# Expert rows written in 512-byte pieces and read in 2 KB pieces, late weight splits in an expert's first unit, and another order of splits and routing in the first unit

## The chip, the cores and the metric

The kernel runs on one core of a Trainium2 chip. The engines that matter here are PE (matmuls), ACT and DVE (elementwise work), POOL (gathers and scatters by index) and SP (which here issues the ordinary DMAs). Each of them takes its instructions in the order in which they stand in its own program. The metric is the device time of one execution in microseconds (us): the median of three runs before was 791.21 us (790.51 to 791.55).

## The reference

Linear attention over 8 batches x 8 heads x 576 positions x 64, then a mixture of experts over the 4608 rows of 512 that the attention gives. Each row goes to the one expert with the highest cosine similarity:

```python
expert_idx = np.argmax(logits, axis=1)
gate_w = probs[np.arange(N), expert_idx]
for e in range(E):
    mask = expert_idx == e
    if not mask.any():
        continue
    h = np.maximum(x[mask] @ w1[e], 0.0)          # 512 -> 1024
    out[mask] = gate_w[mask, None] * (h @ w2[e])  # 1024 -> 512
```

With the given inputs the reference sends 540, 5, 574, 0, 1152, 1759, 0 and 578 rows to the experts 0 to 7.

## The kernel before, in words

**Attention** fills the first 300 us or so. It is followed by the **experts**, in units of at most 384 rows, all of one expert. The order of the experts is worked out on the chip: the largest expert goes first, then the others in cyclic order. Here that gives unit 0 (384 rows of expert 5), units 1 to 5 (the rest of expert 5), 6 and 7 (expert 7), 8 and 9 (expert 0), 10 (the 5 rows of expert 1), 11 and 12 (expert 2) and 13 to 16 (expert 4). Unit 0 is written out (`first_unit`, `first_layers`) and is interleaved with the last routing steps. Every other unit is one of 14 **arms** of a switch (`ARMS`, L33): a size, whether the unit is the first of its expert, whether it is the last. Engines jump into an arm at the unit's start and out of it near its end; the rest of the unit (`unit_end`) is common to all arms. So unit 10 is the only one here whose arm is both first and last. Its 5 rows are computed 256 wide in the first layer (L760) and as two slots in the second.

**Precision.** Weights and rows are held as a high and a low part. `wsplit(0, c)` splits chunk c of 8 of w1, `wsplit(1, c)` chunk c of w2: ACT copies the raw weights `w1r` or `w2r` into the high part, DVE subtracts (L586 to L591). Layer 1 of a chunk is 12 matmuls (L696), followed by a relu on ACT (`high`, L698) and a subtraction on DVE (`low`, L701) that free its PSUM bank; five banks take turns. Layer 2 is three matmuls a slot and chunk (L718).

**Weights.** A first unit (t > 1) asks at chunk 1 for the second half of w1 and the first half of w2 of the next expert, and at chunk 5 for the second half of w2 (L765 to L771). A last unit asks for the first half of w1 of the expert after that (`next_w1`, L721). A last unit splits the next expert's w1 chunk by chunk as its own layer 1 leaves them free (L776, c from 2 to 9) and w2's chunks 0 to 3 (L796, c from 5 to 8); w2's chunks 4 to 7 are split in the expert's first unit (L763). Arms that are not last carry tiny instructions in the same places instead (`idle`, L808), on DVE and ACT.

**Rows.** The rows of unit t+2 are gathered by POOL into `raw` (`collect`, three gathers at chunks 0 to 2), written by SP to the DRAM tensor `xr` (`put`, chunk 4) and read back in another order into `xg` (`fetch`, chunk 7), which needs `put` to have landed. In the next unit, at chunks 5 and 6, DVE transposes `xg` in 32 x 32 blocks into `xt` (`turned`, L626), and `xsplit` makes the high and low parts of the rows for the unit after. `put` is one DMA with runs of 2 KB; `fetch` is four DMAs, one for each group of 32 partitions, with runs of 512 bytes.

**Unit 0.** Three of w1's chunks (5 to 7) are split in `first_layers` at c = 0, 1, 2 (`w1_chunk`, L733). The last routing steps stand at numbered places of the same loop (`extras`, L1052): `norms` at 0, `logits` at 2, `choice` at 4, and at 9 `rest`: `count` (four small matmuls on PE, L434 and L435), `ranks`, `tables` (which unit is which arm), then w2's chunks 4 to 7, the table scatters, and the gathers for unit 1. In this part the order on ACT, DVE, POOL and SP is chosen when the program is built, by the order in which the work is written and by planned costs; only PE's order is written by hand. Within the arms all orders are written by hand.

Of the kernel before, what the change touches and what calls it, by code (L numbers as in the profile page):

```python
# [20 lines left out]
P = 128  # L21
B, H, S, HD = 8, 8, 576, 64
K = 3
# [8 lines left out]
LAG, CUT = 5, 5  # L32
# [80 lines left out]
class Kernel:  # L113
# [382 lines left out]
    def tables(self):  # L496
# [4 lines left out]
        v, cst, tab = self.v, self.cst, self.tab  # L501
        pool = self.pb
        it, ie = cst[:, C_IT:C_IT + 1], cst[:, C_IE:C_IE + E]
        es = self.es

        def t_(name, shape, dt_=F32):
            return pool.tile([P] + shape, dt_, name="t_" + name)

        ci, hi = t_("ci", [E], I32), t_("hi", [E], I32)
        s, c, half, odd, one, nu, few = (t_(n, [E]) for n in ("s", "c", "half", "odd", "one", "nu", "few"))  # L510
# [29 lines left out]
        def one_hot(name, t):  # L540
            a, b = t_(name + "a", [E]), t_(name, [E])
            v.tensor_scalar(out=a, in0=cum, scalar1=t, scalar2=None, op0=ALU.is_gt)
            v.scalar_tensor_tensor(out=b, in0=st, scalar=t, in1=a, op0=ALU.is_le, op1=ALU.mult)
            return b

        def pick(name, m, vals):
            a, r = t_(name + "a", [E]), t_(name, [1])
            v.tensor_tensor(out=a, in0=m, in1=vals, op=ALU.mult)
            v.tensor_reduce(out=r, in_=a, axis=AX.X, op=ALU.add)
            return r  # L550
# [22 lines left out]
        mn = one_hot("mn", ce)  # L573
        v.tensor_copy(out=tab[:, 2:3], in_=pick("nx", mn, ie))
        mn = one_hot("mo", pick("cf", mn, cum))
        v.tensor_copy(out=tab[:, 0:1], in_=pick("ny", mn, ie))

# [27 lines left out]
            self.after(ins, first, mybir.DependencyClass.Sync, "spread over the unit")  # L607

    def put(self, t):
        self.nc.sync.dma_start(out=self.rowsd(t).rearrange("(s p) d -> p s d", p=P), in_=self.raws)  # L610

    def fetch(self, t):

        rows = self.rowsd(t).rearrange("(s i) (g d) -> g i s d", i=32, g=4)
        for g in range(4):
            self.nc.sync.dma_start(out=self.xgs[32 * g:32 * g + 32].rearrange("i s (q d) -> i (s q) d", q=4), in_=rows[g])

    def ordered(self, slots, engines):

# [107 lines left out]
    def first_layers(self, n, extra):  # L727

        self.late_tiles()
        for c in range(8 + LAG):  # L730
            late = c - LAG + 1
            if c < 8:
                self.w1_chunk()  # L733
                if c < 4:
                    self.wsplit(1, c, self.nc.gpsimd)
                hidden = self.layer1(0, c, n, c % 2 if c > 1 else 2 + c)
                if c == 4:
                    self.after(hidden[1], self.counts, mybir.DependencyClass.NoSync, "the count is waited for")
            extra(2 * c)
            if late == 6:  # L740
                self.arms = {1: self.arm(1)}
                self.ordered(3, [self.act_copy, self.dve_copy, self.act_copy])
                self.tc.switch_hint(self.arms[1], len(ARMS), label="unit1")
            if late >= 7:
                self.xtr(1, 3, range(3 * late - 21, min(3 * late - 18, 4)))
            if late > 0:
                self.layer2(late - 1, n, range(3))
            extra(2 * c + 1)

    def layers(self, t, n, first, e):  # L750

        nxt = t + 1 < NU
        slots = range(-(-n // P))
        for c in range(8 + CUT):
            if c < 8:
                hidden = self.layer1(t, c, max(n, 2 * P), (8 * t + c) % 5)  # L760
                if c >= CUT and not self.folded(n):
                    self.idle(self.v)
                if first and 1 <= c < 5:  # L763
                    self.wsplit(1, c + 3)
                if first and c == 1:  # L765
                    new = self.reg(t - 1, 0, [ET.SP], 0, E - 1)
                    for which, half in ((0, 1), (1, 0)):
                        ins = self.wload(which, new, half)
                        self.after(ins, hidden[1], mybir.DependencyClass.Sync, "the arms' code first")
                if first and c == 5:  # L770
                    self.wload(1, new, 1)  # L771
                if c < 3 and t + 2 < NU:
                    self.collect(t + 2, c, hidden[0])
                if c == 4 and t + 2 < NU:
                    self.put(t + 2)
            if 2 <= c < 10:  # L776
                if e is not None:
                    self.next_w1(c - 2, e)
                elif c >= CUT:
                    self.idle(self.v, self.nc.scalar)  # L780
            if c == LAG and nxt:
                self.ahead(t)
            if c == 6 and nxt:
                if e is not None:
                    self.turned([2])
                else:
                    self.idle(self.v)
            if c == 7 and t + 2 < NU:
                self.fetch(t + 2)
            if 6 <= c < 9 and nxt:  # L790
                self.xtr(t + 1, 2 + (e is not None), ([0], [1, 2], [3])[c - 6])
            if LAG <= c < LAG + CUT:
                self.layer2(c - LAG, n, slots)
                if n == P and c == LAG:
                    self.layer2(0, 2 * P, [1])
                if c - LAG < 4:  # L796
                    if e is not None:
                        self.wsplit(1, c - LAG)
                    else:
                        self.idle(self.v, self.nc.scalar)  # L800
        for c in range(CUT, 8):
            self.layer2(c, n, slots[2:])
        if n > 2 * P:
            self.output(t, n, 2)
        if not self.folded(n):
            self.idle(self.v, *[self.nc.scalar] * (1 + (n <= 2 * P)))
# [168 lines left out]
    def build(self):  # L975
        nc, tc, v = self.nc, self.tc, self.v
# [27 lines left out]
        with tc.manual_schedule(engines={ET.PE}):  # L1004
            for q in range(NQ + 1):
                self.quad(q)
            pa.close()
            self.expert_tiles(self.ctx.enter_context(tc.tile_pool(name="wp", bufs=1, reuse_waits="tile")))
            while self.sends:
                self.sends.pop(0)()  # L1010
            self.num(j, 0, 0)
            self.qtr(j, 3)
            self.num(j, 0, 1)
            self.norm(j, 0)
            self.ordered(K, [self.act_copy, self.dve_copy, self.act_copy])
            self.w1_chunk()
            self.qtr(j, 4)
            self.close_np.close()
            pool = self.ctx.enter_context(tc.tile_pool(name="accp", bufs=1, space=PSUM, reuse_waits="tile"))
            self.acc = [self.bk[5]] + [pool.tile([P, 512], F32, name=f"acc{i}") for i in range(1, 3)]  # L1020
            self.num(j, 1, 0)
            self.xtr(0, K)
            self.num(j, 1, 1)
            self.norm(j, 1)
            for i in range(5):
                self.square()
            lo, hi = ([f for f in x if f] for x in (self.steps[:-7], self.steps[-7:]))
            for f in lo:
                f()
            while self.sends:  # L1030
                self.sends.pop(0)()

            def rest():
                for f in hi[3:]:
                    f()
                self.tables()
                for c in range(4, 8):
                    self.wsplit(1, c)
                while self.sends:
                    self.sends.pop(0)()  # L1040
                self.slot_rows(1, self.reg(1, None, [ET.SP], 0, ROWS - 3 * P))
                self.slot_rows(2, self.reg(2, None, [ET.SP], 0, ROWS - 3 * P))
                self.slot_rows(3, self.reg(3, None, [ET.SP], 0, ROWS - 3 * P))
                self.gather(1, self.xd, range(3))

            def loads():
                e = self.reg(0, 2, [ET.SP], 0, E - 1)
                for half, i in ((0, 0), (0, 1), (1, 0), (1, 1)):
                    ins = self.wload(i, e, half)
                    self.after(ins, self.last, mybir.DependencyClass.Sync, "the tokens first")  # L1050

            extras = {0: hi[0], 2: hi[1], 4: hi[2], 9: rest, 15: loads}  # L1052
            self.first_unit(lambda i: extras.get(i, lambda: None)())
            with tc.manual_schedule(engines={ET.Activation, ET.DVE, ET.Pool, ET.SP}):
                self.units(1)
# [19 lines left out]
```

## Time and profile before

| what | value |
|---|---|
| median of the runs | 791.21 us (790.51 to 791.55) |
| the profiled execution's own time | 791.06 us |
| its span, first to last instruction | 789.3 us |
| mean granted PE clock | 0.984 |
| ACT busy, DVE busy | 370.9 us (47%), 438.0 us (56%) |
| POOL busy | 150.3 us (19%) |

The rows of a timeline read: start, duration, engine, source line, operation, what it writes and reads, and in brackets how long the engine had been idle and what released it. In the answer on waits a row reads: who waited, for whom, total us, how often, the longest. "issue" stands for a wait that no semaphore explains. `bk` is a PSUM bank, `hh`/`hl`, `qp` and `q` are high and low parts of the hidden layer's chunks.

### The profile page before, as it was taken

To read this page: it belongs to the slowest core of one execution; us is meant where nothing else is said; L and a number is where in the kernel's file an instruction comes from. 1 tells how busy PE (TensorE), PEld (TensorE's weight loads), DVE (VectorE), ACT (ScalarE), POOL (GpSimd) and SP (SyncE) were. 2 spreads that over 40 slices of the span, in tenths; PEclk is the share of its full clock that TensorE was granted. 3 is DMA by queue.
4 is the path that set the end of the run, shared out by engine and by line. 5 is a ranking of instruction groups with operands and counts; after the bars stand their busy time and mean duration, and the time that the engine had idled before them with its cause. 6 is when DMAs were issued, how large, how long until landed. Compare 5 with 4: busy or idle time off the path is not lost. (4 is left out here: it accounts for less than half of the span.)

```text
span 789.3 us, 23676 instructions
## 1 busy us (share of the span) xinstructions
PE 751.2 (95%) x9492; PEld 678.0 (86%) x9492; DVE 438.0 (56%) x1185; ACT 370.9 (47%) x922; POOL 150.3 (19%) x149
## 2 busy tenths in 40 slices
PE   5999999999999998899999999998999699999995
PEld 5999999999999997888799988887898489889994
DVE  5677797779777976852233235435465454533231
ACT  3556576666666664813233244334354434423232
POOL 1000002100310134342122221122022113203221
PEclk9999999999999998999999999999999799999998
DMA  8545464545545471229565346836946873674453
GB/s 329 185 135 195 142 214 134 189 153 186 186 169 175 162 269 44 68 45 331 153 177 150 118 115 169 281 98 164 271 136 207 243 266 99 201 250 135 146 147 81
DMA packets 81197, 136.47 MB, mean 173 GB/s; under 512 B 14199, under 2 KB 40695, under 8 KB 80832
## 3 DMA queue, kind: packets, MB, share of 16 engines
q1 hardware_dynamic: 71872, 108.05, 43.4%
q0 software_dynamic: 8800, 24.46, 10.2%
q8 instruction: 116, 1.90, 1.0%
q14 instruction: 249, 2.04, 0.9%
q10 hardware_dynamic: 160, 0.02, 0.0%
HBM read 99.50 MB, written 33.59 MB: 169 GB/s over the span
## 5 line engine op out<-in xcount | busy, mean ns | idle before, releaser
L230 DVE TENSOR_REDUCE m<-bk 128x4 f32<-128x512 f32 (+1 forms) x160 | 94.2, 631 | 44.3 <-PE bk L222 44.2
L696 PE MATMUL bk<-x,w1h 128*128 128x256 f32 (+3 forms) x512 | 103.7, 297 | 1.7 <-issue 1.7
L238 ACT ACTIVATE qp<-bk 128x512 f32<-128x512 f32 x128 | 69.2, 592 | 71.8 <-PE bk L264 65.5
L701 DVE SCALAR_TENSOR_TENSOR hl<-bk,hh 128x256 fp32r<-128x256 f32 (+2 forms) x51 | 22.0, 449 | 143.7 <-ACT hh L698 85.0
L296 PE MATMUL bk<-va,kp 128*64 128x73 f32 x2560 | 94.4, 229 | 1.3 <-issue 1.2
L827 POOL DMA_INDIRECT out<-o,ent x40 | 40.0, 1000 | 287.7 <-ACT o L822 186.4
L696 PE MATMUL bk<-xh,w1h 128*128 128x256 f32 (+3 forms) x288 | 86.2, 299 | 5.9 <-issue 4.7
L296 PEld LDWEIGHTS bk<-va,kp 128*64 128x64 f32 x2560 | 87.2, 137 | 3.0 <-issue 2.5
L696 PEld LDWEIGHTS bk<-x,w1h 128*128 128x128 f32 x512 | 83.8, 189 | 5.3 <-issue 3.4
L696 PE MATMUL bk<-xh,w1l 128*128 128x256 f32 (+3 forms) x288 | 85.5, 297 | 0.0
L696 PE MATMUL bk<-xl,w1h 128*128 128x256 f32 (+3 forms) x288 | 85.2, 296 | 0.0
L238 ACT ACTIVATE kp<-d 128x512 f32<-128x512 f32 x128 | 70.0, 619 | 29.3 <-DVE d L232 29.3
L232 DVE TENSOR_TENSOR d<-bk,m 128x512 f32<-128x512 f32 x128 | 81.9, 682 | 0.0
L696 PE MATMUL bk<-x,w1l 128*128 128x256 f32 (+3 forms) x256 | 76.2, 298 | 0.0
L323 PE MATMUL np<-kvs,qp 128*64 128x73 f32 x1984 | 74.3, 228 | 0.6 <-DVE x L346 0.6
L323 PEld LDWEIGHTS np<-kvs,qp 128*64 128x64 f32 x1984 | 69.2, 138 | 1.3 <-DVE x L346 1.0
L698 ACT ACTIVATE qp<-bk 128x256 fp32r<-128x256 f32 (+4 forms) x68 | 27.8, 411 | 77.5 <-PE bk L696 59.7
L696 PEld LDWEIGHTS bk<-xh,w1h 128*128 128x128 f32 x288 | 54.9, 191 | 9.1 <-issue 6.3
L604 POOL DMA_INDIRECT raw<-xd,ent x51 | 52.8, 1035 | 49.1 <-issue 14.1
L718 PE MATMUL acc<-w2h,qp 128*128 128x512 f32 (+2 forms) x172 | 62.1, 395 | 0.0
L718 PE MATMUL bk<-w2h,qp 128*128 128x512 f32 x136 | 51.0, 396 | 6.2 <-ACT qp L698 5.9
L696 PEld LDWEIGHTS bk<-xl,w1h 128*128 128x128 f32 x288 | 55.1, 191 | 1.0
(212 smaller groups left out, 1438.6 us busy)
## 6 DMA issues: line engine op xcount, KB each, us to landing
w1r<-w SPq DMA_DIRECT2D x14, 1024.0 KB
w2r<-w SPq DMA_DIRECT2D x14, 1024.0 KB
xr<-raw SPq DMA_DIRECT2D x17, 768.0 KB
xg<-xr SPq DMA_DIRECT2D x68, 192.0 KB
va<-va SPq DMA_DIRECT2D x16, 730.0 KB
vt<-vT SPq DMA_DIRECT2D x16, 640.0 KB
kt<-kT SPq DMA_DIRECT2D x15, 576.0 KB
qt<-qT SPq DMA_DIRECT2D x15, 576.0 KB
```

What stands on the lines that cost most here:

```text
L230: v.tensor_reduce(out=m, in_=ps, axis=AX.X, op=ALU.max, apply_absolute_value=True)
L232: self.shift = self.pace = v.tensor_tensor(out=d, in0=ps, in1=m.unsqueeze(2).broadcast_to([P, k, P]), op=ALU.subtract)
L238: ins = self.nc.scalar.activation(out=out[:, s], in_=in_, func=AF.Exp, scale=sc)
L296: nc.tensor.matmul(out=self.bk[5][a:a + 64, c0:c0 + W], lhsT=k[:, a:a + 64], rhs=self.va[j][:, 5 * X + i, e], start=(i == 0), stop=(i == 4))
L323: nc.tensor.matmul(out=n[64 * a:64 * a + 64, i * W:(i + 1) * W], lhsT=q, rhs=self.kvs[src, X][:, e, s], start=(s == 0), stop=(s == 1))
L604: ins = self.nc.gpsimd.indirect_dma_start(out=self.raws[:, i], out_offset=None, in_=self.xd, in_offset=bass.IndirectOffsetOnAxis(ap=self.e ...
L696: nc.tensor.matmul(out=ps, lhsT=w[:, d, fs], rhs=x[:, d, :n], start=(d == 0 and i == 0), stop=(d == 3 and i == 2))
L698: high = nc.scalar.activation(out=hh[:, :n], in_=ps, func=AF.Relu)
L701: low = self.v.scalar_tensor_tensor(out=out, in0=ps[:, cs], scalar=0.0, in1=hh[:, cs].bitcast(F32), op0=ALU.max, op1=ALU.subtract)
L718: self.nc.tensor.matmul(out=self.acc[i][:h.shape[1]], lhsT=h, rhs=w[:, c], start=(c == 0 and k == 0), stop=(c == 7 and k == len(parts) - 1))
L827: ins = nc.gpsimd.indirect_dma_start(out=self.ap["out"], out_offset=bass.IndirectOffsetOnAxis(ap=ent[:, 1:2], axis=0), in_=o, in_offset=No ...
```

## The change

- `put` becomes four DMAs, one for each group of 32 partitions, with runs of 512 bytes; `fetch` stays four DMAs but now reads runs of 2 KB. What `xg` holds at the end is the same.
- In arms that are first, `next_w1` (or the tiny instructions) covers only chunks 0 to 3 (c from 2 to 5). Chunks 4 to 7 of w1 and 0 to 3 of w2 are split at c = 8 and 9, behind all of the unit's layer 1. Arms that are not last now carry 12 tiny pairs there, not 9.
- In unit 0, w1's chunks 5 to 7 are split at c = 2, 3, 4; `logits` and `choice` move from places 2 and 4 to 5 and 6; DVE's part of w2's chunks 4 to 7 is ordered behind the last instruction of `tables`.

```diff
     def put(self, t):
-        self.nc.sync.dma_start(out=self.rowsd(t).rearrange("(s p) d -> p s d", p=P), in_=self.raws)
+        rows = self.rowsd(t).rearrange("(i k) (q d) -> q i k d", i=32, q=4)
+        for q in range(4):
+            self.nc.sync.dma_start(out=rows[q], in_=self.raws[32 * q:32 * q + 32].rearrange("i s (g d) -> i (s g) d", g=4))
     def fetch(self, t):
-        rows = self.rowsd(t).rearrange("(s i) (g d) -> g i s d", i=32, g=4)
-        for g in range(4):
-            self.nc.sync.dma_start(out=self.xgs[32 * g:32 * g + 32].rearrange("i s (q d) -> i (s q) d", q=4), in_=rows[g])
+        rows = self.rowsd(t).rearrange("(i s g) c -> g i s c", s=K, g=4)
+        for i in range(4):
+            self.nc.sync.dma_start(out=self.xgs[32 * i:32 * i + 32], in_=rows[i])
...
             if c < 8:
-                self.w1_chunk()
+                if 2 <= c < 5:
+                    self.w1_chunk()
...
-            if 2 <= c < 10:
+            if 2 <= c < (6 if first else 10):
                 if e is not None:
                     self.next_w1(c - 2, e)
-                elif c >= CUT:
+                else:
                     self.idle(self.v, self.nc.scalar)
...
-                if c - LAG < 4:
-                    if e is not None:
-                        self.wsplit(1, c - LAG)
+                late = {8: ((0, 4), (0, 5), (1, 0)), 9: ((0, 6), (0, 7), (1, 1), (1, 2), (1, 3))}.get(c, ()) if first else ((1, c - LAG),) * (c - LAG < 4)
+                for which, k in late:
+                    if e is None:
+                        self.idle(self.v, self.nc.scalar)
                     else:
-                        self.idle(self.v, self.nc.scalar)
+                        self.wsplit(which, k)
...
                 for c in range(4, 8):
-                    self.wsplit(1, c)
+                    high, low = self.wsplit(1, c)
+                    self.behind(low, self.listed)
...
-            extras = {0: hi[0], 2: hi[1], 4: hi[2], 9: rest, 15: loads}
+            extras = {0: hi[0], 5: hi[1], 6: hi[2], 9: rest, 15: loads}
```

`self.listed` is the last instruction of `tables` (L576); `behind` only fixes the order on the engine.

More of the change, by code (lines that the diff above doesn't have):

```diff
@@ L575, in tables @@
         mn = one_hot("mo", pick("cf", mn, cum))
-        v.tensor_copy(out=tab[:, 0:1], in_=pick("ny", mn, ie))
+        self.listed = v.tensor_copy(out=tab[:, 0:1], in_=pick("ny", mn, ie))
     def wload(self, which, e, half):
```

## The prediction, made before the result was known

> **What bounds the kernel now.** I first read the page's head for the span, then the waits of PE from 296 us on, the start of the experts. (The chain of waits helps little: it follows POOL through the last units.)
>
> ```profile
> span 789.3 us, 23676 instructions
> ```
>
> ```profile
> PE bk L696 <- issue: 6.5, 7, 2.4
> PE bk L718 <- ACT qp L698: 5.9, 1, 5.9
> PE bk L718 <- ACT q L698: 1.8, 1, 1.8
> PE bk L696 <- DVE hl L701: 1.2, 1, 1.2
> PE bk L434 <- DVE r_rc L431: 1.0, 1, 1.0
> ```
>
> PE is the bound: these five rows hold almost all that it waits for in 490 us. Two waits for relus come from one place. PE's timeline there (unit 10, the 5-row expert) and the granted clock:
>
> ```profile
> 612.47 0.39 PE L718 MATMUL bk<-w2l,qp 128*128 128x512 f32 x1
> 612.70 0.39 PE L718 MATMUL bk<-w2h,qp 128*128 128x512 f32 x1
> 618.98 0.80 PE L718 MATMUL bk<-w2h,qp 128*128 128x512 f32 x1 [5.90 <-ACT qp L698]
> ...
> 627.28 0.46 PE L696 MATMUL bk<-x,w1h 128*128 128x320 f32 x2
> 627.57 0.31 PE L696 MATMUL bk<-x,w1l 128*128 128x320 f32 x1
> 627.72 0.45 PE L696 MATMUL bk<-x,w1h 128*128 128x320 f32 x2
> ```
>
> ```profile
> 544.00:548.00 4.00, 3.85 (x18) 3.85 (x19) 0.22 (x1) 1.10 (x3) 2.02 (x2) 0.61 0.43 136
> 620.00:624.00 4.00, 2.25 (x6) 1.29 (x6) 3.41 (x8) 2.98 (x7) 0.00 (x0) 0.50 1.02 314
> ```
>
> The third number from the right is the clock. Matmuls follow each other every 0.23 us before the wait, and one takes 0.80 behind it: PE loses the wait, and then runs at half clock. Who holds up the relu, on ACT's timeline:
>
> ```profile
> 618.03 0.63 ACT L208 ACTIVATE w2h<-w2r 128x512 fp32r<-128x512 f32 x1 [10.56 <-DMA w2r<-w]
> 618.57 0.37 ACT L698 ACTIVATE qp<-bk 128x256 fp32r<-128x256 f32 x1
> ...
> 623.58 0.62 ACT L208 ACTIVATE w2h<-w2r 128x512 fp32r<-128x512 f32 x1
> 624.10 0.62 ACT L208 ACTIVATE w1h<-w1r 128x512 fp32r<-128x512 f32 x1
> ...
> 626.07 0.42 ACT L814 ACTIVATE spare<-cst 1x1 f32<-1x1 f32 x2
> 627.56 0.69 ACT L822 ACTIVATE o<-bk,ent 128x512 f32<-128x512 f32 x1 [1.07 <-PE acc L718]
> 628.15 0.68 ACT L822 ACTIVATE o<-acc,ent 128x512 f32<-128x512 f32 x1
> ```
>
> ACT stands 10.56 us at the split of w2's chunk 0, whose weights this same unit ordered; the relu of chunk 6 is queued behind it, chunk 7's behind the next splits. SP's queue shows why the weights are late:
>
> ```profile
> 587.37 0.38 SPq L610 DMA_DIRECT2D xr<-raw  x1
> 588.02 0.38 SPq L584 DMA_DIRECT2D w1r<-w  x1
> 593.17 3.09 SPq L616 DMA_DIRECT2D xg<-xr  x4
> 605.63 0.22 SPq L595 DMA_DIRECT2D ent<-tbl  x1
> 606.81 0.40 SPq L584 DMA_DIRECT2D w1r<-w  x1
> 607.42 0.37 SPq L584 DMA_DIRECT2D w2r<-w  x1
> ```
>
> In unit 9 SP waits for `put` to land (587.37 to 593.17), issues `fetch` until 596.26, and issues nothing for 9.4 us while it goes through two jumps into unit 10. So `put` stands in series ahead of unit 10's weights.
>
> **The change, part by part.**
>
> *Late splits (unit 10).* Eight splits, each an ACT and a DVE instruction, move behind all relus. Then relus 6 and 7 are queued only behind `xsplit`'s copies, whose rows have long been fetched. `unit_end` has 3 chunks x 2 slots x 3 = 18 matmuls; three had run by 612.70. The other 15 at 0.23 end at 612.70 + 0.23 + 3.45 = 616.4; before, unit 11 began at 627.28. That is 10.9: waits of 7.65 and the rest half clock. The jump into unit 11, hidden behind the stall before, now counts: 6.5 us of issue waits over 16 jumps is 0.4 each; I take 0.5, bounds 0 and 2.4 (the longest). Net **-10.4**, and unit 11 begins at 616.9.
>
> The wait does not vanish, it moves. ACT now stands at c = 8 until w2's first half lands (call it L), with the outputs and unit 11's relus queued behind. From L on: six splits 0.52 apart (623.58 to 624.10), 3.1; idles 0.4; two outputs 0.59 apart, 1.2; relu about 0.4, DVE's subtraction about 0.5: unit 11's first PSUM bank is free at L + 5.6. PE needs it after five chunks of layer 1; three matmuls take 0.44 (627.28 to 627.72), a chunk 1.76, so at 616.9 + 8.8 = 625.7. PE waits only if L > 620.1; L was 618.03.
>
> *`put` and `fetch`.* L moves with `put`. No row shows a DMA write of 512-byte runs; the nearest are the read of such runs and the old write, both in units 1 and 2:
>
> ```profile
> 385.02 1.30 DVE L626 STREAM_TRANSPOSE xt<-xg 128x512 f32<-128x512 f32 x2 [10.05 <-DMA xg<-xr]
> ```
>
> ```profile
> 376.66 1.87 SPq L616 DMA_DIRECT2D xg<-xr  x4
> 379.92 0.41 SPq L595 DMA_DIRECT2D ent<-tbl  x1
> 387.45 0.38 SPq L610 DMA_DIRECT2D xr<-raw  x1
> 391.60 2.38 SPq L616 DMA_DIRECT2D xg<-xr  x4
> ```
>
> The same 768 KB take 8.4 us in four DMAs of 512-byte runs (376.66 to 385.02, where DVE is released) and 4.15 as one write of 2 KB runs (387.45 to 391.60, where SP is released). Three more issues are 1.5 (1.87 against 0.38). So the new `put` takes between 5.65 and 8.4. I take 7.0, the middle: 2.85 more. All of SP's later steps in units 9 and 10 shift by it, L becomes 620.9, and PE waits 0.8 at unit 11: **+0.8**, bounds 0 (L = 619.5) and 2.2 (L = 622.3). Next in SP's queue are unit 12's `put` and `fetch`, also some 3 us later; their first user is DVE's transpose in unit 11's chunk 5, at 616.9 + 6 x 1.76 + 0.8 = 628 or later, and what PE needs of the DVE work behind it (the subtraction of chunk 6) comes only after about five chunks' worth of layer 2 with three slots, so some 10 us of cover are left.
>
> The Trainium skill, page "DMA: Bandwidth & Descriptors", section "Rules for kernel authors", speaks against this part: it says not to cut a transfer by groups of partitions, since the parts share the same DMA engines, and to use one transfer over 128 partitions. By that rule the new `put` costs the three issues and gains nothing, 5.65, L is 619.5 and the sum 0.8 lower; the 8.4 of unit 1 (in a stretch with other traffic) says that it can be dearer.
>
> The faster read pays elsewhere: unit 1's DVE waited 10.05 us for `fetch`, and PE did not wait for it. `put` +2.85 and `fetch` -2.7 (8.4 to 4.15 + 1.5) cancel; **0**. In the other units no transpose waits for `fetch` at all; the three issues are SP's time, under PE.
>
> *Unit 0.* DVE's timeline, and the group of w2 subtractions between 330.5 and 336 us:
>
> ```profile
> 330.68 0.17 DVE L416 TENSOR_SCALAR r_rn<-r_rn 128x5 f32<-128x5 f32 x1 [1.15 <-POOL r_rn L412]
> ...
> 331.96 0.55 DVE L701 SCALAR_TENSOR_TENSOR hl<-bk,hh 128x384 fp32r<-128x384 f32 x1
> ```
>
> ```profile
> L591 DVE TENSOR_TENSOR w2l<-w2r,w2h 128x512 fp32r<-128x512 f32 x3 | 2.0, 675 | 0.0
> ```
>
> DVE stood 1.15 us at `logits`, waiting for POOL, ahead of the subtraction that frees PE's bank: PE's wait of 1.2. With `logits` behind that subtraction and w1's splits later this wait should go. Then PE reaches the count 1.2 earlier. `choice`'s result (L431) comes up to 2.0 earlier, without the three w2 subtractions, but w1's splits and other subtractions now lie beside it; of the second wait (1.0) I take 0.3 as gained. **-1.5**; bounds -2.2 and, if a late w1 split (0.7) gets ahead of the count, +0.7. The w2 subtractions now run behind `tables`, 4 x 0.675 = 2.7 on a DVE whose next work for PE is the rows of unit 1, several us later; cover gone, they cost up to 2.7.
>
> *Idles.* Three more tiny pairs in each arm that is not last, between relus, on engines busy half the time: 0.
>
> **Sum**, against the profiled execution's own 791.06 (span 789.3 plus 1.8 around it; the median, 791.21, is 0.15 above): 791.06 - 10.4 + 0.8 - 1.5 = 779.96. I forecast **780.0**; its own range from the bounds is 778 to 784.
>
> **Rivals.**
> *B, the wait comes back at unit 11.* Either L is late or PE's jump is slow, since DMA is full there (share 1.02 at 620 to 624). For: the longest issue wait was 2.4, and clock 0.61 over 4 us (544 to 548) was lost in that place, 1.6 more. Against: L has 2 us to spare at the old landing. With 2.4 for 0.5 and 1.6 of clock on top, plus L one microsecond later than I take: 780 + 1.9 + 1.6 + 1.0 = 784.5. The Trainium skill, page "TensorE: Matmul & The Clock Gate", Part 1, says that the clock falls after an idle window of about 3.4 us; by that rule a 2.4 us wait costs no clock and B is 782.9. The row of 544 to 548 disagrees here.
> *C, more is gained.* PE's issue waits shrink too, as `fetch` loads the DMA engines with fewer packets at the unit's end. Against: nothing shows that `fetch` causes them. Half of 6.5 and the 1.6 of clock: 775.
> *D, slower: the small writes.* Place: SP's wait for `put`, in front of unit 10's weights and of unit 2's rows. If `put` takes p, unit 11 gives back p - 6.2, and unit 1 up to p - 6.9 (4.15 + 2.7), if its DVE work has no time to spare. The gain of 11 is gone at p = 12; at p = 16 the time is 780 + 9.8 - 0.8 + 9.1 = 798.1. For: no such write is in the trace. Against: the read of the same runs takes 8.4.
> *E, the late splits do not pay.* The arm runs, the stall goes, but units 11 and 12 stand for weights and rows that SP asks for no sooner; only unit 0 gains: 789.5. Decides if unit 12's `fetch` lands some 10 us after its first use.
>
> **How the numbers follow.** Forecast 0.60, B 0.19, C 0.09, D 0.05, E 0.07. The range 775 to 787 takes in forecast, B and most of C, and leaves out D, E and the rest of C, under 2 in 10. 0.2% is 1.6 us, about what a measurement of this kernel can tell from no change. Faster by more: forecast, B, C and about half of E, 0.92; within: 0.03; slower: 0.05.
>
> **What would show it.** Right: ACT's long wait for w2r stands behind both relus of unit 10; PE has no wait for relus near 613, and the clock there stays at 1.0; unit 11's first matmul comes some 10 us sooner after unit 10's; SP's `put` to `fetch` is about 7 us; PE's wait at L696 for DVE in unit 0 is gone. Wrong: a new PE wait of several us at unit 11's sixth chunk (B), transposes waiting for `fetch` in many units (D, E), issue waits well under 6.5 (C).

## The result, and the profile after

The changed kernel takes 797.59 us (median of 20 runs) against 792.03 for the kernel before in the same comparison: ratio 1.0062, 95% interval 1.0041 to 1.0084. Four of the 20 runs were slow ones (one took 1470.17 us); every ratio here and below goes by fast runs alone. The changed kernel is slower by 0.6%, where 780.0 and a range of 775 to 787 were forecast. The profiled execution of the changed kernel took 800.23 us, 2.6 above its median, so the 9.2 us between the two profiled executions (800.23 and 791.06) overstate the loss: the ratio is worth 4.9 us.

The page's head and the waits of PE from 296 us on, of the changed kernel (two lines lower in the code than before: L696 is now L698, L718 is L720):

```profile
span 798.3 us, 23837 instructions
```

```profile
PE bk L698 <- issue: 17.2, 9, 5.4
PE bk L720 <- DVE w1l L591: 1.1, 1, 1.1
PE bk L720 <- ACT spare L818: 1.0, 1, 1.0
...
PE bk L698 <- DVE hl L703: 0.7, 2, 0.5
```

The waits for relus (5.9 and 1.8 before) are gone, and unit 0's wait for DVE fell from 1.2 to 0.5 or less. In their place the wait that no semaphore explains went from 6.5 us to 17.2. All nine stand ahead of the first matmul of a unit, where PE jumps into an arm. But 6.5 is a low value even for the kernel before: its second profile (c0, below) has

```profile
PE bk L696 <- issue: 11.9, 7, 2.9
```

Where the time went, by units (from one unit's first layer-1 matmul in PE's timeline to the next unit's; unit 16 to PE's last matmul):

| unit | before, us | after, us | difference |
|---|---|---|---|
| 0 | 39.33 | 37.82 | -1.51 |
| 1 | 32.43 | 33.19 | +0.76 |
| 2 to 4 | 68.02 | 68.30 | +0.28 |
| 5 to 9 | 134.12 | 147.47 | +13.35 |
| 10 | 30.79 | 24.67 | -6.12 |
| 11, 12 | 52.27 | 53.66 | +1.39 |
| 13 to 16 | 100.72 | 100.71 | 0 |

The loss lies in units 5 to 9, which were predicted at 0. (They take 137.25 us in c0, against which the loss is 10.2.) The largest single piece is the jump from unit 5 into unit 6. SP's timeline and PE's first matmul, before:

```profile
473.84 0.37 SPq L610 DMA_DIRECT2D xr<-raw  x1
474.48 0.38 SPq L584 DMA_DIRECT2D w1r<-w  x1
478.15 1.86 SPq L616 DMA_DIRECT2D xg<-xr  x4
```

```profile
486.75 0.42 PE L696 MATMUL bk<-xh,w1h 128*128 128x352 f32 x1 [1.82 <-issue]
```

The same, after:

```profile
474.05 3.05 SPq L612 DMA_DIRECT2D xr<-raw  x4
477.37 0.75 SPq L584 DMA_DIRECT2D w1r<-w  x1
480.12 2.50 SPq L618 DMA_DIRECT2D xg<-xr  x4
```

```profile
490.77 0.65 PE L698 MATMUL bk<-xh,w1h 128*128 128x352 f32 x1 [5.45 <-issue]
491.22 0.49 PE L698 MATMUL bk<-xl,w1h 128*128 128x352 f32 x1
```

The weights that stand behind `put` in SP's queue are asked for 3.3 us after it starts and not 0.64, and `fetch` 6.1 us and not 4.3. PE then waits 5.45 us, not 1.82. Instructions were on their way in that time: the DMA answer for the 10 us around this jump, after (one digit or number of the first two rows is 0.25 us; q14 and q8 are the queues that the profile calls "instruction"), shows

```profile
DMA  9999999999999998889997433611002013000100
GB/s 360 369 344 360 393 369 369 393 213 131 147 156 139 131 156 123 131 189 287 262 205 131 90 123 148 172 57 57 8 33 16 8 16 82 8 0 16 33 0 0
...
q14 instruction: 8, 0.07, 2.3%
q8 instruction: 1, 0.02, 0.8%
```

The window begins at 481 us. The DMA engines are full with the program's own packets until about 486.5, and PE's first matmul comes 4 us behind that. For 2 us from 483.25 on only 123 to 156 GB/s pass, although the engines are as busy as before. This is `fetch` in its new form: the weights are 512 packets of 2 KB and `fetch` is 384, and 537 of these 896 had started by 483.

The packet records show what the wait hangs on. One packet of 16 KB of q8 starts at 487.43, when the other traffic has thinned out. That is 2.1 us after PE's last matmul of unit 5 ended (485.32), and 3.3 us before the next one begins. Before the change the same packet starts at 483.79, which is 1.1 us ahead of the end of PE's last matmul (484.93) and 3.0 us before the next. Over all 18 profiles there are 84 jumps at which PE waited over 0.7 us; in 81 of them the last q8 packet starts 2.5 to 3.9 us before the unit's first matmul, in the other three up to 4.7. So PE's wait ends some 3 us behind this packet, and in the changed kernel the packet is late, behind full engines. (The record doesn't say which engine a packet of q8 is for; that it is PE's code is read from the spacing.)

The windows of the changed kernel show what PE lost besides (the third number from the right is the clock):

```profile
488.00:490.00 2.00, 0.00 (x0) 0.00 (x0) 0.00 (x0) 0.00 (x0) 0.00 (x0) 0.66 0.12 22
490.00:492.00 2.00, 1.23 (x4) 1.24 (x5) 0.00 (x0) 1.26 (x2) 0.47 (x1) 0.50 0.10 23
492.00:494.00 2.00, 2.00 (x9) 2.00 (x8) 0.00 (x0) 0.00 (x0) 1.54 (x2) 0.50 0.45 131
494.00:496.00 2.00, 2.00 (x10) 2.00 (x9) 0.52 (x1) 0.46 (x1) 0.00 (x0) 0.63 0.43 151
496.00:498.00 2.00, 2.00 (x15) 2.00 (x14) 0.39 (x1) 0.89 (x2) 1.14 (x2) 1.00 0.12 14
```

Ten matmuls in 2 us at half clock, 15 at full: so this jump cost its wait and then some 4 us at half clock. Over units 5 to 9 the bracketed waits of PE's timeline add up to 13.4 us after (5.45, 0.22, 2.68, 3.23, 1.83) and 5.1 before. The other 5 us are clock: by the clock records half clock cost PE 7.1 us in these units after, and 1.7 before.

Unit 10 in ACT's timeline, after:

```profile
623.53 0.38 ACT L700 ACTIVATE qp<-bk 128x256 fp32r<-128x256 f32 x1 [1.93 <-PE bk L698]
...
625.67 0.39 ACT L700 ACTIVATE q<-bk 128x256 fp32r<-128x256 f32 x1
...
628.63 0.63 ACT L208 ACTIVATE w2h<-w2r 128x512 fp32r<-128x512 f32 x1 [0.30 <-DMA w2r<-w]
```

Both relus run before the split of w2, and ACT waits 0.30 us there, not 10.56. PE's timeline of the same unit:

```profile
628.38 0.39 PE L720 MATMUL bk<-w2l,qp 128*128 128x512 f32 x1
629.90 0.50 PE L720 MATMUL bk<-w2h,qp 128*128 128x512 f32 x1 [1.13 <-DVE w1l L591]
```

```profile
632.79 0.39 PE L720 MATMUL acc<-w2h,q 128*128 128x512 f32 x1
634.91 0.55 PE L698 MATMUL bk<-x,w1h 128*128 128x320 f32 x2 [1.73 <-issue]
```

The stall is gone; a wait of 1.13 for DVE's splits of w1 and a jump of 1.73 stand in its place.

### The profile page after: what moved, and what is told of

It reads as the page before. It is cut to its first block, busy times and chain, and to the rows that moved or that the text cites. A ratio compares the mean times of both kernels' runs of the same rounds, so it can differ in the third digit from the quotient of the medians.

```text
span 798.3 us, 23837 instructions
## 1 busy us (share of the span) xinstructions
PE 756.1 (95%) x9492; PEld 683.7 (86%) x9492; DVE 439.0 (55%) x1218; ACT 375.1 (47%) x955; POOL 148.9 (19%) x149
## 5 line engine op out<-in xcount | busy, mean ns | idle before, releaser
L698 PE MATMUL bk<-x,w1h 128*128 128x256 f32 (+3 forms) x512 | 105.2, 300 | 6.8 <-issue 6.8
L698 PE MATMUL bk<-xh,w1h 128*128 128x256 f32 (+3 forms) x288 | 88.6, 308 | 11.1 <-issue 10.4
L698 PEld LDWEIGHTS bk<-x,w1h 128*128 128x128 f32 x512 | 84.9, 191 | 10.7 <-issue 8.9
L698 PE MATMUL bk<-xh,w1l 128*128 128x256 f32 (+3 forms) x288 | 87.5, 304 | 0.0
L698 PE MATMUL bk<-xl,w1h 128*128 128x256 f32 (+3 forms) x288 | 87.3, 303 | 0.0
L698 PE MATMUL bk<-x,w1l 128*128 128x256 f32 (+3 forms) x256 | 76.8, 300 | 0.0
L698 PEld LDWEIGHTS bk<-xh,w1h 128*128 128x128 f32 x288 | 56.9, 198 | 14.5 <-issue 12.0
L720 PE MATMUL acc<-w2h,qp 128*128 128x512 f32 (+2 forms) x172 | 61.2, 390 | 0.0
L698 PEld LDWEIGHTS bk<-xl,w1h 128*128 128x128 f32 x288 | 57.3, 199 | 1.0
L698 PEld LDWEIGHTS bk<-xh,w1l 128*128 128x128 f32 x288 | 56.7, 197 | 0.0
```

Of the source, the lines that this page charges most:

```text
L698: nc.tensor.matmul(out=ps, lhsT=w[:, d, fs], rhs=x[:, d, :n], start=(d == 0 and i == 0), stop=(d == 3 and i == 2))
L720: self.nc.tensor.matmul(out=self.acc[i][:h.shape[1]], lhsT=h, rhs=w[:, c], start=(c == 0 and k == 0), stop=(c == 7 and k == len(parts) - 1))
```

## The experiments

Each ratio is to the kernel before, run beside it on the same chip; "issue" is PE's wait of that name from 296 us on. The experiments ran in four groups (e1 to e4, e5 to e8, e9 to e11 with c0, e12 to e15); the kernel before had medians of 791.64, 784.31, 786.64 and 785.27 in them, so ratios can be compared across groups and times cannot. A ratio can differ a little from the quotient of the two medians (e12: 0.9883, and 0.9903 by medians).

### The change taken apart

**e1, the rows as before.** The changed kernel with the old `put` and `fetch`.

```diff
-        for q in range(4):
-            self.nc.sync.dma_start(out=rows[q], in_=self.raws[32 * q:32 * q + 32].rearrange("i s (g d) -> i (s g) d", g=4))
+        self.nc.sync.dma_start(out=self.rowsd(t).rearrange("(s p) d -> p s d", p=P), in_=self.raws)
...
+            self.nc.sync.dma_start(out=self.xgs[32 * g:32 * g + 32].rearrange("i s (q d) -> i (s q) d", q=4), in_=rows[g])
```

> The changed kernel with put and fetch as before (one write of 2 KB runs, four reads of 512-byte runs); late splits and unit 0 stay changed. Theory R (the new rows' DMAs lie on the code that the engines load at a unit's end): PE's issue waits from 296 us on fall from 17.2 to about 6.5, unit 10 takes 21 to 25 us against 30.8 before, and the time is 780 to 785, a ratio of 0.985 to 0.991. Theory C (the arms' own changed programs, with 12 tiny pairs for 9, make the jumps slower): issue waits stay near 17 and the time near 797.

Measured: 790.52 us, ratio 0.9986 [0.9956, 1.0016]; issue 15.2 us. The loss is gone with the rows, and so is all of the gain that was forecast from the rest. Neither theory had expected this: the waits are near theory C's 17, and the time is neither's. Of the 15.2 us, 4.7 stand at one jump, into unit 11, where the old stall had hidden it; at the jumps into units 6 to 10 the waits are 7.1 us, against 13.4 in the changed kernel.

**e2, the rows alone.** The kernel before with only the new `put` and `fetch`.

> The kernel before with the new put and fetch alone. Theory R: issue waits of 15 or more in units 5 to 9, unit 10's stall stays and begins later, 803 to 808, a ratio of 1.014 to 1.020. Theory C: as before, 791 to 793, issue waits near 6.5.

Measured: 802.31 us, 1.0122 [1.0071, 1.0174]; issue 12.9, and 5.7 more at L698 for DVE. The rows alone cost 1.2% (1.4 to 2.0% had been expected), by the middle values twice the whole change.

**e3, unit 0 alone**, and **e4, the late splits alone**, each on the kernel before:

```diff
...
-                self.w1_chunk()
+                if 2 <= c < 5:
+                    self.w1_chunk()
...
-            extras = {0: hi[0], 2: hi[1], 4: hi[2], 9: rest, 15: loads}
+            extras = {0: hi[0], 5: hi[1], 6: hi[2], 9: rest, 15: loads}
```

```diff
-            if 2 <= c < 10:
+            if 2 <= c < (6 if first else 10):
...
+                late = {8: ((0, 4), (0, 5), (1, 0)), 9: ((0, 6), (0, 7), (1, 1), (1, 2), (1, 3))}.get(c, ()) if first else ((1, c - LAG),) * (c - LAG < 4)
...
```

> The kernel before with the changes to unit 0 alone (w1's chunks 5 to 7 at c = 2 to 4, logits and choice later, w2's subtractions behind the tables). Both theories: unit 0 takes 1.5 us less, 37.8 against 39.3, the rest as before: ratio 0.997 to 0.999. If the new order of unit 0 is what disturbs the later units, the ratio is above 1.0.

> The kernel before with the late splits alone. Theory R: unit 10 takes 21 to 25 us against 30.8, issue waits near 6.5, 782 to 786, ratio 0.987 to 0.993. Theory C: issue waits rise to 15 or more and the ratio is 1.0 or above.

Measured: e3 791.0 us, 0.9995 [0.9965, 1.0024]; e4 792.88 us, 0.9997 [0.9976, 1.0018]. In e3's trace unit 0 takes 38.07 us, 1.26 less than in the profile of before: the gain is there, and 0.2% of the time is too small to see in the ratio. e4's unit 10 takes 25.06 us, 5.7 less than in the profile of before, and yet the time is the same, where 0.987 to 0.993 had been expected. That asks what unit 10 takes in other executions of the old arms; see c0.

The jumps tell the rows apart from the rest, over more than one profile. At the jumps into units 6 to 10 PE waits 5.2 to 8.3 us in the five profiles with the old rows in their old places (before, c0, e1, e3, e4), and 9.9 to 14.1 in the three with `put` in four parts and four reads there (the changed kernel, e2, and e5 below). Units 5 to 9 take 134.1 to 139.0 us in the five and 139.6 to 149.2 in the three. In unit 4 `put` has its four parts too, but no weights stand behind it: the wait at the jump into unit 5, another arm, is 0.2 to 0.6 us in the five and 0 to 1.3 in the three.

### What about the rows costs

**e5, `put` cut in four, all else as before.** The runs stay 2 KB long and the reads stay as they were, so neither the small writes nor the new reads are there.

```diff
-        self.nc.sync.dma_start(out=self.rowsd(t).rearrange("(s p) d -> p s d", p=P), in_=self.raws)
+        rows = self.rowsd(t).rearrange("(s q i) d -> q i s d", i=32, q=4)
+        for q in range(4):
+            self.nc.sync.dma_start(out=rows[q], in_=self.raws[32 * q:32 * q + 32])
```

> The kernel before, its write cut into four DMAs of 32 partitions with runs of 2 KB as before; fetch as before. Theory J: what SP has in flight at a unit's end holds up the code that the engines load for their jumps. J1, the three more issues (SP's weight loads come 1.5 to 2.7 us later and so nearer to the jump): ratio 1.005 to 1.012, issue waits 12 or more. J2, the small runs of the write, or J3, the 2 KB reads into groups of 32 partitions: ratio 0.998 to 1.003.

Measured: 794.85 us, 1.0123 [1.0088, 1.0157]; issue 15.5. That is the loss of e2 again, with runs of 2 KB: the cut costs, and a cost of the small runs is not seen (the two intervals leave room for some 0.6%). SP's timeline of e5 at the end of unit 5, and the first row of PE's waits:

```profile
468.38 2.19 SPq L612 DMA_DIRECT2D xr<-raw  x4
470.83 0.59 SPq L584 DMA_DIRECT2D w1r<-w  x1
473.53 2.34 SPq L618 DMA_DIRECT2D xg<-xr  x4
```

```profile
PE bk L698 <- issue: 15.5, 7, 5.0
```

The weights follow 2.45 us after the start of `put` (0.64 before), so 1.8 later; `fetch` follows after 5.15 (4.31 before). The Trainium skill, page "DMA: Bandwidth & Descriptors", section "Rules for kernel authors", says not to cut a transfer by groups of partitions, since the parts go to the same engines. This run agrees that nothing is won by it; here the cut costs 1.2%.

**e6, one read.** The changed kernel with the rows ordered so that each partition's three are neighbours, and `fetch` as one DMA over 128 partitions with runs of 6 KB.

```diff
...
-        for i in range(4):
-            self.nc.sync.dma_start(out=self.xgs[32 * i:32 * i + 32], in_=rows[i])
+        self.nc.sync.dma_start(out=self.xgs, in_=self.rowsd(t).rearrange("(p s) c -> p s c", s=K))
```

> The changed kernel with another order of the rows in DRAM, so that fetch is one DMA over 128 partitions with 6 KB runs; the write stays four DMAs of 512-byte runs. J3 (2 KB packets into 32 partitions took 0.25 us each at 483 us of the changed kernel, against 0.08 for those into 128): fetch lands about 3 us sooner, the ratio falls from 1.006 to 0.990 to 0.998. J1 or J2: it stays at 1.003 to 1.008.

Measured: 785.62 us, 1.001 [0.9982, 1.0037]; issue 7.9. The DMA answer for 10 us from 472 on, e6, with one `fetch` issued at 472.07:

```profile
GB/s 377 369 311 344 369 418 393 123 344 352 393 410 393 467 369 303 156 98 49 33 49 0 25 0 0 33 33 66 33 0 0 33 33 0 0 33 0 0 0 213
```

At first the rest of the weights passes as well. From 474.5 on the packets are nearly all the read's: 300 to 470 GB/s pass, and its bulk is through at 476. The four reads of the changed kernel went at 123 to 156 GB/s for 2 us at this place, and the old ones, with runs of 512 bytes, at 156 to 256 (before, 480.6 to 484). So the new reads are slower than the old ones though their runs are four times longer. Some 0.5% of the time hangs on the shape of the read (1.0062 against 1.001, give or take 0.3%); 0.8 to 1.6% had been expected. e6 differs in three things, 128 partitions for 32, one DMA for four and 6 KB for 2 KB, and does not say which of them counts.

e6 also bounds what e5 says. Its `put` is still cut in four, and yet PE's waits at the jumps into units 6 to 10 are 5.9 us, as with the old rows. By this profile the cut costs where the reads behind it still fill the engines at the jump, and not of itself. If the new reads cost 0.5% by themselves, e2 should be dearer than e5, and it is not; their intervals are too wide to settle that.

**e7 and e8, `fetch` behind the jump.** `fetch` is moved from the end of a unit to the start of the next one: e7 in the changed kernel, e8 with the old rows (e1 with this move).

```diff
+            if c == 0 and t > 1 and nxt:
+                self.fetch(t + 1)
...
-            if c == 7 and t + 2 < NU:
-                self.fetch(t + 2)
```

> The changed kernel with fetch moved from chunk 7 to the start of the next unit, behind SP's own jump. Theory J with fetch as the load that matters: issue waits from 296 us on fall from 17.2 to 6 or less and the ratio is 0.980 to 0.992. If it is the write and the weights behind it (J1, J2): issue waits of 10 or more stay and the ratio is 1.000 to 1.006. If the jumps do not depend on DMA traffic at all: no change, 1.006.

> The old rows (one write of 2 KB runs, four reads of 512 bytes) with the late splits and unit 0 as changed, and fetch moved to the start of the next unit. Theory J: issue waits 6 or less against 15.2 without the move, ratio 0.975 to 0.988. If the jumps do not depend on what fetch moves: 0.998 as without the move.

Measured: e7 784.8 us, 0.9991 [0.9959, 1.0022]; e8 779.73 us, 0.9923 [0.9891, 0.9955]. With either shape the move gains 0.6 to 0.7%: `fetch` in flight at the jump has a price, before the change too. This is less than was expected of a load that matters alone (e8: 0.975 to 0.988). e7's issue waits (14.4) stay long, so `fetch` is not all that the jump meets.

### Is it the weights?

Up to here two causes were open: the weights, asked for 1.8 to 2.7 us later and so in flight nearer to the jump, with `fetch` behind them; or `put` itself, which lands later and holds back `fetch`.

**e9, the store behind the weights.** The changed kernel, `put` moved from chunk 4 to chunk 5, behind that chunk's weight loads. The weights come sooner by this, `put` and `fetch` later.

```diff
-                if c == 4 and t + 2 < NU:
-                    self.put(t + 2)
...
+            if c == 5 and t + 2 < NU:
+                self.put(t + 2)
             if c == LAG and nxt:
                 self.ahead(t)
```

> The changed kernel, with the store of the rows (put) moved from chunk 4 to chunk 5, behind the weight loads of that chunk; nothing is left out. Theory 1 (the three added issues hold back the weights, and the jump then meets them in flight): the weight load is issued some 2 to 3 us sooner than in the changed kernel, PE's issue waits from 296 us on fall from 17 to under 12 us, and the ratio to the kernel before is 0.995 to 1.001. Theory 2 (the store's landing and the fetch behind it are what costs): the store now lands later, the fetch with it, and the ratio is 1.006 to 1.012. Theory 3 (only the number of transfers costs, wherever they stand): 1.004 to 1.008.

Measured: 780.88 us, 0.9942 [0.9913, 0.9971]: 1.2% less than the changed kernel (by the two ratios), from an order of issues alone. Theory 1 holds, with a ratio just under its range; theories 2 and 3 had it at 1.004 or above. SP's timeline at the end of unit 5, e9, and the first row of the waits:

```profile
467.80 0.38 SPq L584 DMA_DIRECT2D w1r<-w  x1
468.42 3.78 SPq L612 DMA_DIRECT2D xr<-raw  x4
476.84 3.04 SPq L618 DMA_DIRECT2D xg<-xr  x4
```

```profile
PE bk L698 <- issue: 8.0, 5, 3.6
```

`fetch` is issued 8.4 us after `put` (468.42 to 476.84), and only 3.8 us ahead of unit 6's first matmul at 480.66. The DMA engines are quiet between the two, from about 475 to 478 (the DMA answer's first row, one digit for 0.25 us from 473 on):

```profile
DMA  9999997200000000010215866874558889943799
```

The 16 KB packet of q8 starts in this quiet, at 477.84, 2.0 us before PE's last matmul ends, and PE's wait at this jump is 0.81 us (5.45 in the changed kernel). So the move does two things here: the weights come sooner, and `fetch` starts so late that its packets run behind that of the code.

**e10, without the weights at a unit's end.** The first half of w1 that a last arm loads and the second half of w2 that a first arm loads are left out; the matmuls run on what the buffers hold.

```diff
-        if c == 3:
-            self.wload(0, e, 0)
...
-                if first and c == 5:
-                    self.wload(1, new, 1)
```

> The changed kernel without the weight loads that stand at a unit's end (the first half of w1 that each last arm loads in chunk 3 and the second half of w2 that each first arm loads in chunk 5 are left out; the matmuls run on what the buffers hold, so the same instructions run with fewer transfers). Theory 1 (PE's jump waits behind weights in flight): issue waits of PE from 296 us on fall from 17 us to under 8, and the ratio is 0.975 to 0.985. Theory 2 (store and fetch alone fill the queues at the jump): issue waits stay over 12 us and the ratio is 0.998 to 1.006. Anything between: both share it.

Measured: 773.26 us, 0.9841 [0.9788, 0.9895]; issue 5.7, the longest 1.6. With `put` and `fetch` as in the changed kernel, but without these weights, the waits are shorter than before the change, and 2.2% of the time goes with them. So these weights decide whether the jumps meet full engines. They need not be the packets in flight: at the jump into unit 6 of the changed kernel those were `fetch`'s (above), which the weights had held back.

### The place and the shape, the late splits and the stall

**e11**: the kernel before with e8's move of `fetch` alone. **e12**: e1 (old rows, late splits, unit 0) with e9's move of `put`. **e13**: the kernel before with e9's move of `put` alone. **e14**: the changed kernel with both moves. **e15**: e1 with both moves. **c0**: the kernel before itself, for another profile. The edits are those shown.

> The kernel before, with the fetch of the next rows moved from the end of a unit to the start of the next one, and nothing else. If the move alone makes the gain of the run with old rows, late splits, unit 0's splits and this move (0.9923), the ratio is 0.990 to 0.995; if the late splits and unit 0 add to it once the jump is quiet, it is 0.996 to 1.000.

> The kernel before once more, for another profile of the same program. If the stall of unit 10 (ACT 10.56 us at the wait for w2r, PE 7.7 us behind it) belongs to the program, unit 10 takes 30 to 31.5 us again and ACT's wait is 9 to 11 us; if it is one draw among several, unit 10 takes 24 to 28 or over 32 us, and the lost time stands in other units.

> The changed kernel with the old rows (one store, one 128-partition fetch), the store moved to chunk 5 behind the weight loads. Theory 1 (the place against the weights is the cost; the shape is worth nothing of itself): within 0.3% of the run with the new rows and the same place, so 0.991 to 0.997. Theory 2 (four parts and reads by groups of 32 partitions cost something wherever they stand): 0.986 to 0.991. Theory 3 (the 512-byte rows do gain, once the weights go first): 0.997 to 1.002.

> The kernel before with one move: the store of the rows from chunk 4 to chunk 5, behind the weight loads. Theory 1: one issue of 0.65 us is all that the weights gain, so the ratio is 0.994 to 1.000, nearer 1 than the run with four parts moved stands to the changed kernel. If the store's own traffic, and not its issues, is what the weights wait for, 0.988 to 0.994.

> The changed kernel with both moves: the store behind the weight loads, the fetch at the next unit's start. If the two remove the same wait (PE's at the jump): as good as the store's move alone, 0.991 to 0.996. If each removes a wait of its own: 0.985 to 0.990, and issue waits of PE from 296 us on under 7 us.

> As the run with both moves, but with the old rows. If the shape of the rows is worth nothing: the same ratio as that run within 0.3%. If four parts cost something of themselves: 0.3 to 0.6% less, and it is the fastest of all.

Measured, with the earlier runs in their places:

| `put` and `fetch` at | new rows, late splits, unit 0 | old rows, late splits, unit 0 | old rows, old arms |
|---|---|---|---|
| their old places | 1.0062 [1.0041, 1.0084] | 0.9986 [0.9956, 1.0016] (e1) | 1 |
| `fetch` behind the jump | 0.9991 [0.9959, 1.0022] (e7) | 0.9923 [0.9891, 0.9955] (e8) | 0.9934 [0.9904, 0.9965] (e11) |
| `put` behind the weights | 0.9942 [0.9913, 0.9971] (e9) | 0.9883 [0.9849, 0.9917] (e12) | 0.9960 [0.9932, 0.9987] (e13) |
| both | 0.9882 [0.9843, 0.9921] (e14) | 0.9869 [0.9832, 0.9905] (e15) | not run |

Down a column: each move gains. A difference of two of these ratios is uncertain by some 0.4%, so which move is worth more is not shown. In the first column the two add up (0.7% and 1.2%, together 1.8%), as if they removed different waits. In the second they overlap more (0.6% and 1.0%, together 1.2%). From the first column to the second: the new rows cost 0.6 to 0.8% in three rows of the table (theory 2 of e12) and 0.1%, nothing measurable, where both moves keep the jump clear. They gain nowhere. The issue waits of e14 and e15 (3.9 and 4.7 us) are the shortest of all kernels that compute everything; e14's first rows of the waits:

```profile
PE bk L720 <- ACT x L208: 5.0, 1, 5.0
PE bk L698 <- issue: 3.9, 5, 2.0
```

What is left is unit 10 again, 5.0 us behind an ACT copy of unit 11's rows. DVE's timeline of e14 says why:

```profile
602.41 1.30 DVE L628 STREAM_TRANSPOSE xt<-xg 128x512 f32<-128x512 f32 x2 [6.10 <-DMA xg<-xr]
```

This is what `fetch` behind the jump costs: its rows now come too late in the short unit 10, where nothing waited for them before. e12, e14 and e15 are faster than the kernel before by 1.2 to 1.3%, and so than both kernels.

From the third column to the second: the late splits and unit 0 give 0.1% with `put` ahead of the weights or with `fetch` moved, both within the intervals, and 0.8% where `put` stands behind the weights (e13 and e12, side by side; 0.6% by their medians). e13's profile has the old stall in full:

```profile
PE bk L718 <- ACT qp L698: 6.5, 1, 6.5
PE bk L718 <- ACT q L698: 1.8, 1, 1.8
```

Its unit 10 takes 30.91 us, e12's 25.81. But c0, the very kernel before, takes 25.96 in its second profile, and ACT's wait there is

```profile
ACT w2h L208 <- DMA w2r<-w: 6.8, 1, 6.8
```

not 10.56. In seven profiles with the old arms unit 10 takes 24.2 to 33.0 us; in the ten with late splits that compute everything 24.0 to 26.8. With unit 11, into which the stall is pushed, the means are 58.5 and 56.4 us (55.4 to 63.8, and 54.1 to 57.8). In four of the seven unit 10 takes over 27 us, in none of the ten. So the late splits make unit 10 steadier, and gain 2 us on average in these profiles, not 9.6; the two sets overlap, and their kernels differ in more than the splits. Part of what eats the gain stands at the jump into unit 11, which the stall used to hide: in six of the ten (e1, e4, e8, e9, e12, e15) PE waits 1.8 to 4.7 us there and then loses 1.6 to 3.1 us to half clock. That is rival B, in its own place.

## Why the prediction was wrong, point by point

**The step that failed** is the one that put the rows at 0: "the three issues are SP's time, under PE", and "cancel; 0" for `put` and `fetch` outside unit 10. It looked for who waits for SP's rows, found that no transpose does, and stopped. What waits is PE, for its code: behind `put` in SP's queue stand the weights and `fetch`, all share the DMA engines with the code's packets, and what is asked for later is still in flight at the jump. In place of 0 the rows alone cost 1.2%, some 9.6 us (e2). e5 shows it with the cut alone (1.2%), e9 shows that the order of issues decides (1.2% back), e10 that the engines are clear in time without these weights (2.2%).

By ratios the other terms came to nearly nothing as well: the late splits alone to 0.9997 [0.9976, 1.0018], where 10.4 us were forecast, and unit 0 alone to 0.9995 [0.9965, 1.0024]. So of the some 16 us between the forecast and the result, the price of the rows and the missing gain of the late splits (below) are some 10 us each; the parts do not add up exactly.

The rows of before that told of the rows' price were on the table: issue waits of 6.5 us, DMA share 1.02 ahead of a jump. They were priced at one jump, unit 11's, in rival B. It had the right mechanism, at one place of six and a third of the size: 4.5 us, against 13.35 in units 5 to 9 of these two profiles. Against rival C stood that nothing shows `fetch` to cause these waits; e7, e8 and e11 show that it causes part of them (0.6 to 0.7%), only that the change did not take it away.

**Late splits, -10.4: the relus' stall goes as said; the size is wrong.** ACT's wait stands behind both relus, PE has no wait for them, as said. Unit 10 came to 24.67 us and not to 20.4 (616.9 less 596.49). The 4.3 between: 1.13 waiting for DVE's w1 splits, which were not in the working; a jump of 1.73 where 0.5 was taken; and 1.7 of clock, which falls to 0.5 at the unit's start (the last section). The larger error is in what was saved: the stall of 10.9 was read from one profile as the program's own, and the kernel before also runs unit 10 in 25.96 (c0). And the jump into unit 11, priced at 0.5, took 1.73 here and up to 4.7, with half clock behind it, in other runs. Rival E's outcome, that only some 1.5 us are gained, is about what e1 shows (0.9986), but by this jump and not by late weights and rows.

**L and unit 11, +0.8.** The weights landed 18.4 us into unit 10 (628.63 less 610.23), and 24.4 had been worked out; PE has no wait at unit 11's sixth chunk. This term is 0, within its bounds.

**`put`, 7.0 us: right.** From its first issue to `fetch` it is 6.07 us in unit 5 (rows above) and 7.16 in unit 1 of the changed kernel:

```profile
376.21 2.51 SPq L618 DMA_DIRECT2D xg<-xr  x4
...
386.21 3.06 SPq L612 DMA_DIRECT2D xr<-raw  x4
393.37 3.14 SPq L618 DMA_DIRECT2D xg<-xr  x4
```

Rival D's small writes are thereby refuted: p is 6 to 7, not 12 or 16, and the kernel was slower for another reason.

**`fetch`, -2.7: wrong.** It was to take 5.65 us, as the write of 2 KB runs over all partitions does. DVE's transpose in unit 1 of the changed kernel is released at

```profile
385.29 1.31 DVE L628 STREAM_TRANSPOSE xt<-xg 128x512 f32<-128x512 f32 x2 [11.03 <-DMA xg<-xr]
```

9.1 us after the issue at 376.21 (first row above); it was 8.4 with the old form. The length of the runs was taken for the cause of the old form's slowness. Four times the length in the same groups of 32 partitions did not help; one DMA over 128 partitions with still longer runs did (e6).

**Unit 0, -1.5: right.** That it is right to the hundredth in the trace (39.33 to 37.82) is luck: the means are 39.0 us in the seven profiles with the old unit 0 and 37.9 in the eleven with the new one, so 1.1. PE's two waits fell as said (DVE's subtraction from 1.2 to 0.2, the count from 1.0 to 0.4). **Idles, 0:** not refuted. The one new wait of 1.0 us for ACT's `spare`, in unit 1, is there in e5 too (0.9), whose arms are the old ones.

In sum, the profiled execution came out 20.3 us above the 779.96: 13.35 from units 5 to 9, 4.3 from unit 10, and the other 2.7 from units 1, 4, 11 and 12 and from the attention, which took 0.9 longer with the same code.

What stays open: why the late splits pay 0.8% only where `put` stands behind the weights (e13's stall was seen in one profile of it); and why the losses of the parts do not add up to that of the whole, 1.2% for the rows alone and 0.6% with the rest.

## What to carry to other kernels

Before adding an issue to a queue, look at what is queued behind it and where that will be in flight: here four issues in place of one, with nobody waiting for them, cost 1.2% by pushing the transfers behind them towards a jump, and moving the same four behind the weights gave it back. In a kernel that jumps between programs, keep the DMA queues empty at the jump; issue what must not be late first, and what can wait after the jump. Take a stall that one profile shows for a draw until a second profile shows the same length.

## What the runs showed of the hardware

A jump's price depends on the traffic: PE's wait at the same jump was 0.81 us where the 16 KB packet of q8 found quiet DMA engines (e9) and 5.45 where it stood behind full ones. The Trainium skill, page "Runtime: NRT & Kernel Launch", section "Instruction fetch mechanics", says that a taken branch whose target isn't at hand forces a DMA fetch of the code; the trace agrees, with that packet 3.3 us before the first matmul in the changed kernel and 2.8 in e9.

Four reads of 32 partitions with 2 KB runs passed at 123 to 156 GB/s for 2 us, one read of 128 partitions with 6 KB runs at 300 to 470, from the same DRAM tensor.

The clock fell after short waits. Into unit 10 of the changed kernel PE waited 1.83 us (until 610.23), and then:

```profile
610.00:611.00 1.00, 0.77 (x6) 0.78 (x7) 0.00 (x0) 0.00 (x0) 0.00 (x0) 1.00 0.56 133
611.00:612.00 1.00, 1.00 (x9) 1.00 (x8) 0.00 (x0) 0.00 (x0) 0.00 (x0) 0.76 0.28 82
612.00:613.00 1.00, 1.00 (x6) 1.00 (x6) 0.00 (x0) 0.87 (x2) 0.00 (x0) 0.50 0.08 23
613.00:614.00 1.00, 1.00 (x6) 1.00 (x6) 0.00 (x0) 0.40 (x1) 0.90 (x1) 0.50 0.02 8
614.00:615.00 1.00, 1.00 (x7) 1.00 (x6) 0.00 (x0) 0.00 (x0) 0.69 (x2) 0.53 0.43 143
615.00:616.00 1.00, 1.00 (x10) 1.00 (x10) 0.04 (x1) 0.53 (x2) 0.42 (x1) 1.00 0.51 139
```

Some 3.4 us at half clock, 1.7 us lost, almost as much as the wait itself; a wait of 2.61 in e12 (until 479.50) cost no clock. So the length of a wait alone does not decide.
